# Sending one more batch of strided attention output through DRAM and a DMA transpose, with an earlier deadline

## The chip, the cores and the metric

The kernel runs on one core of a Trainium2 chip. The metric is device time in microseconds. Profiles are single executions. Their times count from the start of the span, which is a little shorter than the timed run. With one core there is no second die to compare with: the label only says that a run took over 1.5% more than the fastest run of the same kernel.

## The reference

Sparse attention with 8 batches, 8 heads, 576 positions and head size 64. Heads 0 to 3 use a local mask, heads 4 to 7 a strided one. Its output x is 4608 x 512 and goes through two matrix products:

```python
rel = pos[:, None] - pos[None, :]
mask_local = (rel >= 0) & (rel < 32)
mask_strided = (rel >= 0) & (pos[None, :] % 32 == pos[:, None] % 32)
attn = softmax(where(mask, q @ k.T / 8, -1e9));  x = attn @ v   # heads side by side
h = x @ w_in            # 512 -> 2048
out = (relu(h) ** 2) @ w_out   # 2048 -> 512
```

## The kernel before

The two-layer part works on chunks of 512 tokens. Each chunk has 16 groups of four matmuls for the first layer (`mm1`) and 16 for the second (`mm2`). From chunk 3 on, the first layer of chunk c alternates with the second layer of chunk c - 1, so a chunk takes 32 groups. Chunk b is the first to need batch b. Attention steps are strewn between the groups so that each batch is done by a deadline. The hooks (`at(n, ...)`) start the loads of later batches at given groups.

A strided unit (two heads) leaves its x with tokens on partitions, and the first layer needs it transposed, in `xt`. The kernel has two ways to do that:

```python
    def step_E(u):                       # on TensorE: 8 transposes, then a copy out of PSUM
        ...
        for t in range(n):
            nc.tensor.transpose(px[:, w * t:w * (t + 1)], x[:, 2 * t:2 * t + 2, :]..., ident[0:w, 0:w])
        dst = xt[p][:, b * S:(b + 1) * S]
        copy = nc.scalar.copy if u < 12 else nc.vector.tensor_copy
        ...
    XD = 6
    def by_dram(u):                      # strided units of batches XD and later
        return not is_local(u) and units[u][0] >= XD

    def step_X(u):                       # by DRAM: write x, six groups later transpose it with a DMA
        b, p = units[u]
        t = dram.tile([S, 2 * D], BF16, name="x_d")
        nc.sync.dma_start(out=t.rearrange("(p j) c -> p (j c)", j=NJ), in_=st.pop(u)["x"]...)
        later(6, lambda: nc.sync.dma_start_transpose(out=xt[p][:, b * S:(b + 1) * S], in_=t))
```

The deadline and the loads hang on the same constant:

```python
    def plan(b, n0, g0, g1):             # loads of batch b; for b >= 4:
        ...
        g = g0 + (g1 - g0) * 45 // 100
        at(g, lambda: loads_qk(b))                                   # q, k and the casts to DRAM
        at(max(g + 8, g0 + (g1 - g0) * 8 // 10), lambda: transpose_str(b))   # L161
        at(n0, lambda: loads_v(b))
        for i in range(2):
            at(g + 14 + 4 * i, lambda u=4 * b + i: transpose_local(u))       # L173
    ...
        g_end, s_end = ready.get(b, starts[b] - (14 if b >= XD else 2)), ends[4 * b + 3]
        ...
        if b + 2 < B:
            plan(b + 2, g_end + 2, g_prev, g_end)
```

So the deadline of batch b also decides when batch b + 2 is loaded. From batch 2 on, the plain q, k and v loads, the x writes, all DMA transposes and all output stores but one last half are issued by SyncE, in program order. The casts of q and k to DRAM and the casts in SBUF are GpSimd's.

The softmax here doesn't subtract the row's maximum and nothing guards it: scores larger than these inputs give would overflow.

Of the kernel before, what the change touches and what calls it, by code (L numbers as in the profile page):

```python
# [14 lines left out]
def kernel(  # L15
# [79 lines left out]
    def is_local(u):  # L95
        return units[u][1] < H // 4
# [356 lines left out]
                                  px.rearrange("c (j p) -> c p j", j=NJ))  # L453
        st.pop(u)

    XD = 6

    def by_dram(u):
        return not is_local(u) and units[u][0] >= XD

# [294 lines left out]
    for b in range(1, B):  # L755
        g_end, s_end = ready.get(b, starts[b] - (14 if b >= XD else 2)), ends[4 * b + 3]
        if b == 1:
# [48 lines left out]
```

## Time and profile before

| | before |
|---|---|
| time, median of 6 runs | 315.38 us (314.51 to 317.44) |
| span of the profiled run | 311.4 us |
| TensorE busy | 96% |
| chain of waits that ended last | TensorE 82%, DMA 7% |

TensorE is the bound, and the DMA engines are nearly full until about 187 us. The lines that carry this are in the prediction. There, ph and py groups are `mm1` and `mm2` (L480 and L498), L444 the x transposes on TensorE, L464 and L466 the x write and its DMA transpose. In SyncE's queue, L107 are the loads of q and k, L185 and L201 the loads of v, L161 the transposes of strided q and k, L173 those of local q and k, L437 those of local x, and L510 the output stores.

### The profile page before, as it was taken

What the parts mean: (1) busy time and instruction counts of PE and PEld (TensorE: products, weight loads), DVE (VectorE), ACT (ScalarE), POOL (GpSimd) and SP (SyncE); (2) the same over time, 40 slices, a digit from 0 to 9 for tenths busy, and PEclk for the clock granted to TensorE, in tenths of its full rate; (3) what the DMA queues carried; (4) which work ended last, traced back from release to release, by engine and by line L of the source; (5) the groups of instructions that cost most, each with busy time, mean ns of one, the idle gap of its engine ahead of it and who ended that gap; (6) DMA issues with size and microseconds to landing.
All of it is one profiled execution on the core that took longest, in us unless ns stands there. A gap on an engine that the chain in (4) does not pass through costs nothing.

```text
span 311.4 us, 6122 instructions
## 1 busy us (share of the span) xinstructions
PE 297.9 (96%) x2309; PEld 147.9 (47%) x2352; DVE 164.5 (53%) x411; ACT 162.8 (52%) x337; POOL 91.5 (29%) x117
## 2 busy tenths in 40 slices
PE   8889989999999999999999999999999999999994
PEld 3444545544555545454454545444444444444441
DVE  6775456468866876577468656654432222222200
ACT  3947746577545765554555565555434444444311
POOL 8527863726830813291048025000000000000000
PEclk9979999999999999999999999999999999999999
DMA  8999999999999999999899886224131000000111
GB/s 148 153 207 204 212 188 257 190 273 232 192 197 222 229 186 170 173 251 226 146 206 196 187 183 132 72 72 55 53 104 56 34 37 34 34 34 36 67 67 67
DMA packets 92172, 44.99 MB, mean 144 GB/s; under 512 B 76592, under 2 KB 85456, under 8 KB 91952
## 3 DMA queue, kind: packets, MB, share of 16 engines
q1 hardware_dynamic: 77120, 34.09, 52.0%
q0 software_dynamic: 14880, 10.39, 23.1%
q8 instruction: 18, 0.29, 0.4%
q10 hardware_dynamic: 144, 0.13, 0.1%
q14 instruction: 10, 0.08, 0.1%
HBM read 36.70 MB, written 13.57 MB: 161 GB/s over the span
## 4 chain that ended last, share of the span: by engine, by line
PE 82%; DMA 7%; POOL 4%; DVE 3%; issue 2%; ACT 1%; DVEq 0%; POOLq 0%
PE ph L480 35%; PE py L498 27%; PE ph L498 11%; DMA w_in_b<-in_moe_w_in_dram 4%; PE pt L412 4%; PE pt L314 3%; DMA qT_s<-in_q_dram 3%; DVE x_s L427 1%; PE pt L270 1%; PE pt L444 1%; POOL w_in_b L233 0%; POOL kT_s L133 0%; DVE kTl L285 0%; POOL w_out_b L237 0%; DVE rinv L426 0%
## 5 line engine op out<-in xcount | busy, mean ns | idle before, releaser
L480 PE MATMUL ph<-xt,w_in_b 128*128 128x512 bf16 x558 | 142.5, 380 | 1.2 <-issue 0.3
L486 ACT ACTIVATE r<-ph 128x512 bf16<-128x512 f32 x143 | 85.3, 597 | 94.4 <-PE ph L480 90.6
L487 DVE TENSOR_TENSOR g_sb<-r 128x512 bf16<-128x512 bf16 x144 | 68.5, 478 | 105.2 <-ACT r L486 104.6
L498 PE MATMUL py<-w_out_b,g_sb 128*128 128x512 bf16 x379 | 99.8, 379 | 1.1 <-issue 0.3
L480 PEld LDWEIGHTS <-w_in_b 128*128 128x128 bf16 x576 | 52.3, 98 | 56.4 <-issue 0.5
L498 PEld LDWEIGHTS <-g_sb 128*128 128x128 bf16 x576 | 52.4, 98 | 55.2
L319 ACT ACTIVATE e<-pt 128x288 bf16<-128x288 f32 (+1 forms) x128 | 47.4, 407 | 13.5 <-PE pt L314 13.4
L498 PE MATMUL ph<-w_out_b,g_sb 128*128 128x512 bf16 x170 | 41.8, 379 | 0.6 <-issue 0.3
L412 PEld LDWEIGHTS <-e 128*128 128x128 bf16 (+1 forms) x392 | 20.9, 97 | 16.2 <-DVE e L325 0.8
L192 POOL CAST vl<-vl_st 128x768 bf16<-128x768 f32 x12 | 11.1, 925 | 50.3 <-DMA vl_st<-in_v_dram 50.1
L427 DVE TENSOR_TENSOR x_s<-pt,rinv 72x384 bf16<-72x384 f32 (+1 forms) x42 | 21.4, 509 | 1.4
L123 POOL CAST q_l<-q_st 96x768 bf16<-96x768 f32 x14 | 13.1, 937 | 24.9 <-DMA q_st<-in_q_dram 24.5
L325 DVE TENSOR_TENSOR e<-e,mask_loc 128x576 bf16<-128x576 bf16 x32 | 18.7, 586 | 2.4 <-ACT e L319 2.4
L509 ACT COPY y<-py 128x512 f32<-128x512 f32 x25 | 14.6, 585 | 5.7 <-PE py L498 5.4
L123 POOL CAST k_l<-k_st 96x768 bf16<-96x768 f32 x14 | 14.3, 1024 | 10.6 <-DMA k_st<-in_k_dram 9.8
L325 DVE TENSOR_TENSOR e<-e,mask_str 72x576 bf16<-72x576 bf16 x32 | 15.5, 490 | 3.1 <-ACT e L319 3.1
L426 DVE RECIPROCAL rinv<-pt 96x6 f32<-96x6 f32 (+2 forms) x70 | 12.8, 183 | 7.9 <-PE pt L412 7.9
L427 DVE TENSOR_TENSOR x_l<-pt,rinv 96x384 bf16<-96x384 f32 x28 | 15.5, 553 | 1.0
L509 ACT COPY y<-ph 128x512 f32<-128x512 f32 x10 | 5.9, 585 | 17.4 <-PE ph L498 17.4
L208 POOL CAST vs<-v_st 72x1024 bf16<-72x1024 f32 x12 | 13.4, 1146 | 0.4
L412 PE MATMUL pt<-vs,e 72*128 72x65 bf16 x224 | 13.1, 193 | 0.1
L523 PE MATMUL py<-y 128*128 128x512 bf16 x22 | 9.6, 523 | 1.3 <-DVE y L652 1.3
(87 smaller groups left out, 159.0 us busy)
## 6 DMA issues: line engine op xcount, KB each, us to landing
out_dram<-y SPq DMA_DIRECT2D x35, 256.0 KB, 3.4
vl_st<-in_v_dram SPq DMA_DIRECT2D x24, 144.0 KB, 3.4
v_st<-in_v_dram SPq DMA_DIRECT2D x12, 288.0 KB
q_st<-in_q_dram SPq DMA_DIRECT2D x16, 144.0 KB, 4.6
k_st<-in_k_dram SPq DMA_DIRECT2D x16, 144.0 KB, 5.8
w_in_b<-in_moe_w_in_dram POOLq DMA_DIRECT2D x4, 512.0 KB, 12.8
w_out_b<-in_moe_w_out_dram POOLq DMA_DIRECT2D x4, 512.0 KB, 10.5
q_st<-in_q_dram SPq DMA_DIRECT2D x7, 288.0 KB, 9.9
```

What stands on the lines that cost most here:

```text
L123: copy(t.rearrange("p j h d -> p h j d"), s[name + "f"].rearrange("p h (j d) -> p h j d", j=6))
L208: (copy or nc.gpsimd.tensor_copy)(t[:, :, 0:D], s["vf"].rearrange("p h (j d) -> p (h j) d", d=D))
L319: nc.scalar.activation(e[0:kn, lo:lo + S // 2], banks[row][half][0:kn, 0:S // 2], AF.Exp, scale=scale)
L325: nc.vector.tensor_tensor(x, x, m.to_broadcast([kn, n, w]), op=ALU.mult)
L412: nc.tensor.matmul(po[:, n - n0, :], e[0:kn, pos(n):pos(n) + 128], rhs[0:kn, src(n), 0:D + 1], start=True, stop=True)
L426: nc.vector.reciprocal(rinv[0:w, 0:m], po[0:w, 0:m, D:D + 1])
L427: nc.vector.tensor_tensor(x, po[0:w, 0:m, 0:D], rinv[0:w, 0:m].to_broadcast([w, m, D]), op=ALU.mult)
L480: nc.tensor.matmul(ph, w_in_b[:, kk, 128 * ff:128 * (ff + 1)], xt[kk][:, 512 * c:512 * (c + 1)], start=(kk == order[0]), stop=(kk == order ...
L486: nc.scalar.activation(r, ph, AF.Relu)
L487: later(1, lambda: nc.vector.tensor_tensor(g[:, ff, :], r, r, op=ALU.mult))
L498: nc.tensor.matmul(py, g[:, ff, 128 * j:128 * (j + 1)], w_out_b[:, ff, :], start=(ff == 0), stop=(ff == 15))
L509: nc.scalar.copy(y, py)
```

## The change

The intent is to take 16 transposes and two copies of batch 5 from TensorE and VectorE. As x then has a longer way, batch 5's attention gets the deadline that batches 6 and 7 have: 14 groups before its chunk instead of 2.

```diff
-    XD = 6
+    XD = 5
```

## The prediction

> **What bounds the kernel now.** I read the page first, then the chain of waits, then TensorE's timeline through the stage of batches 5 and 6, and then the timeline of SyncE's DMA queue over the same stretch. From the page of the kernel before:
>
> ```profile
> span 311.4 us, 6122 instructions
> PE 297.9 (96%) x2309; PEld 147.9 (47%) x2352; DVE 164.5 (53%) x411; ACT 162.8 (52%) x337; POOL 91.5 (29%) x117
> DMA  8999999999999999999899886224131000000111
> L444 PE MATMUL pt<-ident,x_s 72*128 72x72 bf16 x80 | 4.8, 197 | 1.0 <-DVE x_s L427 0.8
> ```
>
> The first two lines say that TensorE is busy 96% of the span. The chain of waits that ended last is 82% TensorE. So an instruction taken from TensorE in the middle of the run is worth its own slot, and no more. The third line has slices of 311.4 / 40 = 7.8 us: the DMA engines are 80 to 90% busy until slice 24, about 187 us. The change works just before that point. The fourth line holds the transposes the change removes (16 of 80, those of batch 5). TensorE's timeline shows what they cost on the path:
>
> ```profile
> 165.56 1.03 PE L498 MATMUL py<-w_out_b,g_sb 128*128 128x512 bf16 x4
> 166.43 0.42 PE L444 MATMUL pt<-ident,x_s 72*128 72x72 bf16 x8
> 166.69 1.03 PE L480 MATMUL ph<-xt,w_in_b 128*128 128x512 bf16 x4
> ...
> 176.55 0.34 PE L412 MATMUL pt<-vl,e 128*128 128x65 bf16 x6
> 176.73 1.03 PE L480 MATMUL ph<-xt,w_in_b 128*128 128x512 bf16 x4
> ```
>
> Columns are start, extent, engine, line, operands, count. Groups of four matmuls start 0.865 us apart (166.43 - 165.56 = 0.87), and a block of eight transposes moves the next group by 166.69 - 166.43 = 0.26 us. There are no holes here. Counted in the built order, the L480 group at 176.73, just after batch 6's first L412 block, is group 144. It is the first of chunk 5, which is the first to read batch 5's x. In the kernel before, the second x copy of batch 5 runs on VectorE from 175.02 to 175.78, just in time for that group's fourth matmul near 177.4, with no DMA. The change puts that x behind SyncE's queue, so that queue decides:
>
> ```profile
> 164.60 1.28 SPq L437 DMA_TRANSPOSE xt<-x_l  x1
> 165.97 0.52 SPq L510 DMA_DIRECT2D out_dram<-y  x1
> 171.12 1.46 SPq L161 DMA_TRANSPOSE qT_s<-q_d  x1
> 172.67 1.58 SPq L161 DMA_TRANSPOSE kT_s<-k_d  x1
> 174.34 0.53 SPq L510 DMA_DIRECT2D out_dram<-y  x1
> 174.97 1.23 SPq L173 DMA_TRANSPOSE qT<-q_l  x1
> ...
> 180.83 2.99 SPq L185 DMA_DIRECT2D vl_st<-in_v_dram  x4
> 183.87 0.90 SPq L201 DMA_DIRECT2D v_st<-in_v_dram  x2
> ```
>
> See the hole from 166.49 to 171.12, then 13 us with hardly a gap. This is batch 7's loading. The queue's own waits over 166 to 172 us name the hole:
>
> ```profile
> SPq L161 <- DMA q_d<-in_q_dram: 4.6, 1, 4.6
> ```
>
> The queue stands still until batch 7's cast of q to DRAM has landed. GpSimd issues that cast at 165.16, only after casting batch 6's v.
>
> **What the Trainium skill says.** "Perfetto Trace Analysis", section "DMA Instruction — HWDGE (DVE, Sync)", puts the semaphore wait in the sequencer before the reported start, and frees it for the next instruction only at the reported end. The trace agrees: nothing was issued in the 4.6 us. "DMA: Bandwidth & Descriptors", section "Two DMAs through the same engine are not ordered", says a DMA that reads what an earlier one wrote must wait for the completion semaphore. The built program has that wait between x's write (L464) and its transpose (L466). The issue times fit but do not show it. "TensorE: Matmul & The Clock Gate", section "What's actually happening", says about 3.4 us of idleness halves the array clock, and about 3.4 us of activity restores it. The trace agrees on the size of a half-clock stretch: TensorE was sparsely used just before 16 us, and granted clock over 16-18, 18-20 and 20-22 us was 0.85, 0.50 and 0.79, which adds up to 3.4 us at half clock:
>
> ```profile
> 18.00:20.00 2.00, 2.00 (x25) 1.27 (x23) 1.59 (x5) 0.70 (x2) 0.34 (x1) 0.50 1.24 206
> ```
>
> (The last three columns are granted clock, DMA share and GB/s.)
>
> **The change part by part.** It removes, for two units of batch 5, 16 transposes and two 128x576 copies. On TensorE that is 2 x 0.26 = 0.52 us on the path. The copies (about 0.75 us each on VectorE, 53% busy) lie beside other work and give nothing.
>
> It adds two writes x_d<-x_s and two transposes xt<-x_d. Batch 6's show SyncE issue times of 0.33 and 1.18 us, and the transpose lands 2.6 us after issue when DMA is quiet. Batch 6's x_l transposes had a median of 5.1 in the busy stretch.
>
> It moves batch 5's attention from groups 110-142 to 110-130, batch 6's from 142-162 to 130-162, and batch 7's loads earlier: q and k from group 124 to 119, their strided transposes from 135 to 127, v from 144 to 132. The squeeze itself costs nothing that I can see: batch 6 has run in 20 groups without a hole. Of batch 6's work, three more product blocks and one more unit's scores now precede group 144: 3 x 0.18 us and one of about 0.5, so 1.0 us. These only move from after it to before it. Group 144 starts near 176.7 - 0.5 + 1.0 = 177.2 us, and its fourth matmul, which needs the second x, 3 x 0.22 later, near 177.9.
>
> Now the built issue order on SyncE, with the waits of the kernel before. The order is unchanged until batch 6's v loads at 155 us. Batch 7's q and k, an output and two x_l transposes follow as before, and the first x write is issued near 165.6. Then the two L161 transposes stand in line **before the second x write**. Their wait is q_d, and GpSimd's order, which sets q_d, has not changed. So the hole still ends near 171.1. From there the queue issues, in this order: two L161, output, second x write, first x transpose, six v loads, two L173, output, and only then the second x transpose. Durations with gaps, from the rows above: 1.55 + 1.67 + 0.61 + 0.40 + 1.25 + 3.04 + 1.00 + 1.32 + 1.32 + 0.60 = 12.76 us. The second x transpose is issued at 171.1 + 12.8 = 183.9. I choose 4.5 us for landing, between 2.6 and 5.1 and near the latter, because the v loads just before it are in flight. So x lands near 188.4.
>
> The stall at group 144 is 188.4 - 177.9 = 10.5 us, on the path, because TensorE takes its matmuls in order. It is longer than 3.4 us, so the array comes back at half clock for about 3.4 us: 1.7 us lost, an estimate from the half-clock stretch above. Sum: 315.67 - 0.5 + 10.5 + 1.7 = 327.4 us.
>
> **The rivals.** *The transfer is hidden, as intended.* Fourteen groups are 14 x about 1 us, and for batch 6 it worked: second write at 196.13, transpose at 202.38, next chunk at 209.08. Against it: batch 6's queue has no later batch to load, while batch 5's stands in batch 7's. This would give 315.67 - 0.5 = 315.2.
>
> *A short stall of 2 to 5 us,* if q_d lands earlier, or the L161 wait falls in a quieter queue. The order is fixed and 12.8 us of issue remain, so the hole would have to end near 165 us, before GpSimd has even issued the cast at 165.16. With 1.7 for the clock, if it is hit at all, this would give 317 to 322.
>
> *A longer stall,* if the DMA engines bind and not the issue. Between 155 and 190 us the hardware queue's packets alone take
>
> ```profile
> q1 hardware_dynamic: 16480, 6.08, 95.2%
> ```
>
> of the 16 engines' time, and the change adds four transfers there. Landing could be 7 or 8 us: 330 to 331.
>
> *VectorE or ScalarE becomes the bound in the squeezed stretch:* about half busy in the page; batch 6 speaks against it. At most 1 us.
>
> **Range and chances.** The predicted time is 327.4 us. The low end, 322.4, is the queue 5 us faster than I add up; the high end, 331.4, is a landing 4 us later. Faster by over 2% (below 309.4) has nothing behind it, as only 0.5 us is removed: 0.01. Within 2% (up to 322.0) needs the stall to be under about 5 us (322.0 - 315.2 - 1.7): 0.11. Slower by over 2%: 0.88.
>
> **What would show it.** Right: TensorE has one hole of 8 to 14 us near 178 us, ahead of an L480 group waiting for DMA xt<-x_d. SyncE shows the L161 wait for q_d of 4 to 5 us ahead of the second L464, and the second batch-5 L466 starts near 184. The clock is 0.5 for about 3.4 us after the hole. L444 falls from 80 to 64, and the page's row of slices has a hole in PE near slice 23. Wrong: if the second L464 is issued before 168 us, or the hole ahead of L161 is gone, the stall shrinks to the first rival's. If TensorE stalls earlier than group 144, an input of batch 5 or 6 was late, and I have missed a wait.

## The result, and the profile after

| | before | after |
|---|---|---|
| time, median of 6 runs | 315.38 us | 326.14 us (324.43 to 328.15) |
| span of the profiled run | 311.4 us | 324.9 us |
| chain of waits: TensorE, DMA | 82%, 7% | 62%, 20% |
| x transposes on TensorE (L444, x_s) | 80 | 64 |

The ratio is 1.0339, with a 95% interval of 1.0285 to 1.0393. Ratios are the mean time of one kernel's fast runs over that of the other's of the same rounds, so not quite the ratio of the medians. From the page of the kernel after:

```profile
PE   8889898999899999999999169999999999999994
PEclk9999999999999999999999859999999999999999
...
L480 PE MATMUL ph<-xt,w_in_b 128*128 128x512 bf16 x572 | 144.9, 381 | 9.9 <-DMA xt<-x_d 9.6
```

Each digit is a slice of 324.9 / 40 = 8.1 us. The 23rd and 24th digits (179 to 195 us) are 1 and 6 in TensorE's row, a hole where 9 is usual, and 8 and 5 in the granted clock. Before the change the L480 row had 1.2 us of idleness and none of it from a DMA; now 9.6 us wait for x's DMA transposes. TensorE's timeline of the kernel after shows where:

```profile
179.08 0.59 PE L480 MATMUL ph<-xt,w_in_b 128*128 128x512 bf16 x2
181.21 0.38 PE L480 MATMUL ph<-xt,w_in_b 128*128 128x512 bf16 x1 [1.53 <-DMA xt<-x_d]
189.67 0.58 PE L480 MATMUL ph<-xt,w_in_b 128*128 128x512 bf16 x1 [8.09 <-DMA xt<-x_d]
190.19 0.70 PE L314 MATMUL pt<-qT_s,kT_s 64*72 64x72 bf16 x16
190.82 1.89 PE L498 MATMUL py<-w_out_b,g_sb 128*128 128x512 bf16 x4
```

One group of four is torn into 2 + 1 + 1. It is group 144, the first of chunk 5. Its third matmul waits for the first strided x of batch 5 and its fourth for the second. Between them TensorE ran nothing: no later matmul overtook the waiting one in those 8.1 us. Afterwards a group takes 1.7 us instead of 0.87 (190.82 to 192.50). SyncE's queue in the same stretch:

```profile
168.19 0.52 SPq L464 DMA_DIRECT2D x_d<-x_s  x1
171.38 2.73 SPq L161 DMA_TRANSPOSE qT_s<-q_d  x1
174.65 1.28 SPq L161 DMA_TRANSPOSE kT_s<-k_d  x1
176.02 0.54 SPq L510 DMA_DIRECT2D out_dram<-y  x1
176.65 0.34 SPq L464 DMA_DIRECT2D x_d<-x_s  x1
177.09 1.20 SPq L466 DMA_TRANSPOSE xt<-x_d  x1
178.38 2.29 SPq L185 DMA_DIRECT2D vl_st<-in_v_dram  x4
180.76 0.85 SPq L201 DMA_DIRECT2D v_st<-in_v_dram  x2
181.73 1.21 SPq L173 DMA_TRANSPOSE qT<-q_l  x1
183.05 1.21 SPq L173 DMA_TRANSPOSE kTl<-k_l  x1
184.68 0.37 SPq L510 DMA_DIRECT2D out_dram<-y  x1
185.11 1.21 SPq L466 DMA_TRANSPOSE xt<-x_d  x1
```

The second x write stands behind batch 7's L161, and its transpose behind six v loads and two L173. The second transpose is issued at 185.11, and TensorE's fourth matmul starts 4.56 us later. The hole, the clock and the removed transposes add up to 9.6 + 1.8 - 0.5 = 10.9 us, where 1.8 is the clock's share, taken from the filled-hole experiment below. The medians differ by 326.14 - 315.38 = 10.8. That this is so close is in part chance: 9.6 is the hole of one profile, and two more profiles of the change (below) have 6.8 and 7.4. The two profiles here differ by more, 13.5 us. Group 144 started at 179.08, and 1.9 us of that is beyond the 177.2 worked out from the profile of before, whose run (313.14 us) was itself 2.2 us faster than its median. The last 0.7 us is not accounted for.

### The profile page after: what moved, and what is told of

The parts are those of the page before. It is cut to its first block, busy times and chain, and to the rows that moved or that the text cites.

```text
span 324.9 us, 6145 instructions
## 1 busy us (share of the span) xinstructions
PE 301.7 (93%) x2336; PEld 147.1 (45%) x2336; DVE 165.3 (51%) x409; ACT 163.0 (50%) x337; POOL 91.4 (28%) x117
## 2 busy tenths in 40 slices
DMA packets 93556, 45.58 MB, mean 140 GB/s; under 512 B 77832, under 2 KB 86696, under 8 KB 93336
## 4 chain that ended last, share of the span: by engine, by line
PE 62%; DMA 20%; POOL 5%; DVE 5%; SPq 3%; issue 2%; ACT 1%; POOLq 0%; DVEq 0%; ACTq 0%
PE ph L480 27%; PE py L498 23%; PE ph L498 8%; DMA vs<-in_v_dram 4%; DMA w_in_b<-in_moe_w_in_dram 4%; DMA qT_s<-in_q_dram 3%; PE pt L314 2%; PE pt L412 2%; DMA k_d<-in_k_dram 2%; DMA vl_st<-in_v_dram 2%; DVE x_s L427 2%; DMA k_st<-in_k_dram 2%; SPq L173 1%; DMA xt<-x_d 1%; DMA kTl<-k_l 1%
## 5 line engine op out<-in xcount | busy, mean ns | idle before, releaser
L480 PE MATMUL ph<-xt,w_in_b 128*128 128x512 bf16 x572 | 144.9, 381 | 9.9 <-DMA xt<-x_d 9.6
L498 PE MATMUL py<-w_out_b,g_sb 128*128 128x512 bf16 x400 | 103.6, 381 | 0.0
L480 PEld LDWEIGHTS <-w_in_b 128*128 128x128 bf16 x576 | 52.7, 98 | 59.2 <-issue 3.4
L498 PE MATMUL ph<-w_out_b,g_sb 128*128 128x512 bf16 x176 | 42.8, 379 | 0.0
L192 POOL CAST vl<-vl_st 128x768 bf16<-128x768 f32 x12 | 11.5, 956 | 53.8 <-DMA vl_st<-in_v_dram 40.1
L325 DVE TENSOR_TENSOR e<-e,mask_loc 128x576 bf16<-128x576 bf16 x32 | 19.6, 613 | 2.4 <-ACT e L319 2.4
L325 DVE TENSOR_TENSOR e<-e,mask_str 72x576 bf16<-72x576 bf16 x32 | 17.1, 540 | 3.1 <-ACT e L319 3.1
L426 DVE RECIPROCAL rinv<-pt 96x6 f32<-96x6 f32 (+2 forms) x70 | 12.8, 182 | 8.9 <-PE pt L412 8.9
L123 POOL CAST k_l<-k_st 96x768 bf16<-96x768 f32 x14 | 13.1, 938 | 8.2 <-DMA k_st<-in_k_dram 8.1
L208 POOL CAST vs<-v_st 72x1024 bf16<-72x1024 f32 x12 | 13.5, 1148 | 0.4
L314 PEld LDWEIGHTS <-kT_s 64*72 64x72 bf16 x192 | 4.6, 118 | 13.7 <-issue 13.1
## 6 DMA issues: line engine op xcount, KB each, us to landing
w_out_b<-in_moe_w_out_dram POOLq DMA_DIRECT2D x4, 512.0 KB, 10.9
```

The costliest lines, as they stand in the source:

```text
L123: copy(t.rearrange("p j h d -> p h j d"), s[name + "f"].rearrange("p h (j d) -> p h j d", j=6))
L208: (copy or nc.gpsimd.tensor_copy)(t[:, :, 0:D], s["vf"].rearrange("p h (j d) -> p (h j) d", d=D))
L325: nc.vector.tensor_tensor(x, x, m.to_broadcast([kn, n, w]), op=ALU.mult)
L426: nc.vector.reciprocal(rinv[0:w, 0:m], po[0:w, 0:m, D:D + 1])
L480: nc.tensor.matmul(ph, w_in_b[:, kk, 128 * ff:128 * (ff + 1)], xt[kk][:, 512 * c:512 * (c + 1)], start=(kk == order[0]), stop=(kk == order ...
L498: nc.tensor.matmul(py, g[:, ff, 128 * j:128 * (j + 1)], w_out_b[:, ff, :], start=(ff == 0), stop=(ff == 15))
```

## The experiments

Two theories stood at first. **Order:** x comes late because of what stands ahead of it in SyncE's queue. **Full engines:** x comes late because the DMA engines have more to move in that stretch, whatever the order. A third suspect was the squeeze of batch 5 into 20 groups.

**The early deadline alone.** The deadline and batch 7's early loads stay, and batch 5's x is transposed on TensorE as before.

```diff
-        return not is_local(u) and units[u][0] >= XD
+        return not is_local(u) and units[u][0] >= 6
```

> The early deadline alone (batch 5's attention in 20 groups, batch 7's loads early), with batch 5's x still transposed on TensorE. Queue theory: no x of batch 5 waits in SyncE's queue, so no hole at group 144; 315 to 316.5 us, within 0.4% of before. Rival (the squeeze or the early loads are what costs): near 326 us, with the hole still there.

Measured: 315.64 us median, ratio 1.0022 (0.9998 to 1.0045). No first-layer matmul waits for x. The squeeze and the early loads cost nothing that can be told from noise.

**Batch 7's loads back at their old groups**, x still by DRAM.

```diff
-            plan(b + 2, g_end + 2, g_prev, g_end)
+            plan(b + 2, *((144, 110, 142) if b == 5 else (g_end + 2, g_prev, g_end)))
```

> The change, but with batch 7's loads put back to the groups at which the kernel before issues them (q and k 124, strided transposes 135, local transposes 138 and 142, v 144). Now both x writes and the first x transpose stand before the two L161 transposes in SyncE's queue; only the second x transpose stands behind them. Queue theory: second x transpose issued about 7 us earlier than in the change (near 177 to 178 instead of 185.1), hole at group 144 of 2 to 4 us in all, 317 to 320 us. Rival (the DMA engines are full, the same bytes move in the same stretch): hole of 7 us or more, 323 us or more.

Measured: 317.74 us median of 12 runs (313.16 to 321.17), ratio of the fast runs 1.0034. The profile fell in a run labelled slow (320.07 us), with one wait of 3.7 us for x. Most of the loss is gone. The second x transpose was issued at 179.87 there, some 2 us later than expected. The runs scatter widely: six of the 12 are slow, and the ratio leaves them out. Whether all six had such a wait is not known, since only one was profiled. So the ratio of the fast runs may flatter this kernel; the median holds all 12.

**The strided transposes behind x as well.** As the last one, and L161 at group 138.

```diff
-        at(max(g + 8, g0 + (g1 - g0) * 8 // 10), lambda: transpose_str(b))
+        at(138 if b == 7 else max(g + 8, g0 + (g1 - g0) * 8 // 10), lambda: transpose_str(b))
```

> As the run with the loads put back, but batch 7's strided transposes L161 at group 138, so that they too stand behind the second x transpose. The bytes are the same. Queue theory: second x transpose issued near 174, landed near 178, hole of 0 to 1 us, 315 to 316.5 us (0.5 us of removed transposes against a rest of the hole). Rival (DMA engines full): still 5 us or more of hole, over 320 us.

Measured: 315.5 us median of 20 runs, ratio 0.9998 (0.9974 to 1.0022). SyncE's queue in this kernel:

```profile
169.23 0.66 SPq L464 DMA_DIRECT2D x_d<-x_s  x1
174.38 1.17 SPq L466 DMA_TRANSPOSE xt<-x_d  x1
...
176.27 1.18 SPq L466 DMA_TRANSPOSE xt<-x_d  x1
177.56 1.32 SPq L161 DMA_TRANSPOSE qT_s<-q_d  x1
```

The second x transpose is issued at 176.27 instead of 185.11 (some 2 us later than expected), group 144 starts at 180.01, and TensorE waits for no x:

```profile
180.01 1.03 PE L480 MATMUL ph<-xt,w_in_b 128*128 128x512 bf16 x4
```

The change and this kernel move the same 45.58 MB in the same 93556 packets. What differs is the order of issue, and with it when each transfer runs, and the loss is gone. That shows the place in the queue as the cause, against the theory that the order does not matter. It does not part SyncE's issue time from the load on the DMA engines: with the v loads, their bytes too went behind x (DMA share over 170 to 180 us 0.71, against 0.99 in the change). The 0.5 us that the removed transposes should bring lies within the interval, so it is neither shown nor excluded. This is the best version with batch 5 by DRAM, and it is level with the kernel before. None of the versions run here beats both.

**The cast earlier.** The wait ahead of L161 is for batch 7's cast to DRAM, so I moved that to the front of GpSimd's order.

```diff
+        if b < 7:                 # in loads_qk
             cast_str_dram(b)
 ...
+        if b == 7:                # in plan
+            at(108, lambda: cast_str_dram(b))
```

> The change with its issue order on SyncE as it is, but batch 7's casts of q and k to DRAM moved to the front of GpSimd's order (group 108, ahead of batch 6's v), so that L161 finds its data landed. Queue theory: the wait of 2.6 us before L161, most of its 2.7 us of issue and the 0.5 us before the second one fall away, 3.5 to 5 us in all, so the hole shrinks from 9.6 to about 5 us: 320 to 322.5 us. Rival (full DMA engines set the landing whatever the issue order): unchanged near 326 us.

Measured: 328.89 us median of 4 runs (327.31 to 329.55), ratio 1.0433. This expectation failed: the kernel is slower than the change. SyncE's queue:

```profile
174.45 0.50 SPq L464 DMA_DIRECT2D x_d<-x_s  x1
175.06 1.30 SPq L161 DMA_TRANSPOSE qT_s<-q_d  x1
...
187.15 1.72 SPq L466 DMA_TRANSPOSE xt<-x_d  x1
```

The wait is gone, exactly as meant: 0.1 us between the first x write and L161. But that write is issued at 174.45 instead of 168.19, 6.3 us later, which is more than the wait was. Batch 6's local transposes began 2.6 us later than in the change (150.91 against 148.32), before the cast can have mattered much: it was issued at 147.71. The queue already lagged at one transpose of a local x (L437), which held it for 5.72 us from 139.65, against 2.70 from 140.14 in the change; why, no run shows. TensorE waited 1.4 us for a local x there, before the cast was issued, so that part of this kernel's time isn't the cast's. The rest came while the cast's transfer ran: those four transposes took up to 2.91 us of issue each, against at most 1.38, and the v loads behind them began at 160.51 instead of 154.34. Here, moving one transfer forward went with everything behind it moving back.

**The cast left out.** To take away both wait and transfer, batch 7's L161 read batch 6's cast. Its output is wrong, which doesn't matter for the time. The comparison with the reference still passed, so its tolerance doesn't see this error.

```diff
+            if b == 7:
+                big[b, name] = kept[name]
+                continue
```

> Wrong result on purpose: the change without batch 7's casts of q and k to DRAM; its strided transposes L161 read batch 6's casts, which landed long before. Wait and transfer are both gone, the order on SyncE is as in the change. If the wait for the cast (2.6 to 5 us in the profiles of the change) was on the path to x: second x transpose near 179 to 181 instead of 183 to 185, hole of 3 to 6 us, 319 to 322.5 us. If the queue was only standing still while the DMA engines worked off their backlog, and the v loads ahead of x are what counts: 323 us or more, as in the change.

Measured: 323.75 us median of 4 runs, ratio 1.0254 (1.0188 to 1.0319). The change, run beside it for the third time (below), had 326.52. From SyncE's queue (line numbers are 4 higher in this kernel):

```profile
168.03 1.45 SPq L468 DMA_DIRECT2D x_d<-x_s  x1
169.57 1.31 SPq L165 DMA_TRANSPOSE qT_s<-q_d  x1
...
181.75 1.16 SPq L470 DMA_TRANSPOSE xt<-x_d  x1
```

No wait, and the second x transpose comes 1.9 us earlier than in the change beside it (183.64), with a hole of 5.1 instead of 7.4 us. By the two medians, the wait and the cast's transfer together are worth 2.8 us. That size is uncertain: the intervals of the two ratios overlap (the change's is 1.0257 to 1.0386), and the change's second repetition, in another round, had 323.81. The result falls between the two theories: the hole (3 to 6 us) is as the first foretold, the time (323 us or more) as the second, and the transpose's issue lies between them. What is clear is that the greater part of the loss remains without them.

**Only the v loads and local transposes behind x.** L161 stays ahead.

```diff
-        at(n0, lambda: loads_v(b))
+        at(138 if b == 7 else n0, lambda: loads_v(b))
 ...
-            at(g + 14 + 4 * i, lambda u=4 * b + i: transpose_local(u))
+            at((140 if b == 7 else g + 14) + 4 * i, lambda u=4 * b + i: transpose_local(u))
```

> The change with batch 7's v loads at group 138 and its local transposes at 140 and 144, so that they stand behind the second x transpose; the L161 transposes and their wait stay ahead of the second x write. Issue-order theory: the second x transpose no longer waits for six v loads and two L173 but only for its own write to land, so it is issued near 181 to 182 instead of 185 and lands near 185 to 186: hole of 5 to 7 us, 321 to 324 us. Rival (only the total of the DMA engines' work up to then counts, not the order): 326 us.

Measured: 316.86 us median of 20 runs (313.77 to 324.04), ratio of the fast runs 1.0035 (1.0009 to 1.0061). Better than I expected (321 to 324 us). Seven of the 20 runs are slow. The profile fell in a run labelled slow, with a wait for x of 4.1 us in two parts, so how the typical run does without is not seen.

**Only L161 behind x.** The line of the strided-transposes experiment alone.

> The change with only batch 7's strided transposes L161 moved behind the second x transpose (group 138); v loads and two L173 stay ahead of it. Issue-order theory: the wait for the cast is no longer ahead of x, but the first x transpose now waits for its write to land, then v loads and L173: second x transpose near 181 to 183, hole of 5 to 8 us, 321 to 325 us. Neither this run nor the one with the v loads moved should reach the 315.5 us of the run with both moved.

Measured: 323.59 us median of 4 runs, ratio 1.0281, hole 7.35 us, second x transpose at 182.05:

```profile
175.10 2.18 SPq L185 DMA_DIRECT2D vl_st<-in_v_dram  x4
...
182.05 1.68 SPq L466 DMA_TRANSPOSE xt<-x_d  x1
```

As expected. Of the two things that stand ahead of x, the v loads and local transposes are the dear ones, and L161 with its wait the cheap one.

**The hole filled with matmuls.** To see the clock's share, 40 matmuls that nobody reads before group 144.

```diff
+    def fill():
+        pw = ps_t.tile([128, 512], FP32, name="pt")
+        for _ in range(40):
+            nc.tensor.matmul(pw, w_in_b[:, 0, 0:128], w_in_b[:, 0, 0:512], start=True, stop=True)
+    at(144, fill)
```

> The change, with 40 matmuls of 128x512 that nobody reads (40 x 0.216 = 8.6 us) on TensorE just before group 144, where it otherwise waits some 9.6 us for x. Clock theory: the wait stays, hidden under them, but TensorE is idle for only about 1 us, so the clock stays at full speed and the 2.1 us lost at half clock after the wait come back: about 2 us less than the change run beside it, granted clock 0.99. Rival (the half clock costs nothing on the path): the same time as the change, or more.

Measured: 325.14 us median of 6 runs, ratio 1.0339. The change beside it:

> The change as it is, beside these runs on the same chip: 324.5 to 328 us, hole of 8 to 11 us at group 144, as measured before.

Measured for the change again (no edit): 323.81 us median of 4 runs (323.66 to 326.44), hole 6.8 us, both a little below what was expected. So the fill saved no time, and the expectation failed as put. In the profiled run of the filled kernel x came later than in the change beside it: its transpose was issued at 185.73 instead of 183.24, and the fourth matmul of group 144 started 1.9 us later (189.04 instead of 187.11), which used up what the clock gave back. Whether the fill or chance made it later is not known; the change's own three profiles spread from 183.2 to 185.1. The timelines still part the two effects. First the filled kernel, then the change again (its lines are numbered one higher):

```profile
179.59 8.80 PE L757 MATMUL pt<-w_in_b 128*128 128x512 bf16 x40
188.22 1.20 PE L480 MATMUL ph<-xt,w_in_b 128*128 128x512 bf16 x4
...
198.03 1.03 PE L480 MATMUL ph<-xt,w_in_b 128*128 128x512 bf16 x4
```

```profile
187.11 0.59 PE L481 MATMUL ph<-xt,w_in_b 128*128 128x512 bf16 x1 [6.84 <-DMA xt<-x_d]
...
197.94 1.03 PE L481 MATMUL ph<-xt,w_in_b 128*128 128x512 bf16 x4
```

Between the fourth matmul of group 144 and the same later group lie 197.94 - 187.11 = 10.83 us in the change, and 198.03 - 189.04 = 8.99 us in the filled kernel (189.04 is the group's end, 188.22 + 1.20, less the 0.38 us of its last matmul; the group lasts 1.20 us instead of 1.03 because that matmul still waited 0.17 us for x). The difference, 1.8 us, is the half clock. Granted clock over the span was 0.997 and 0.977.

**A shorter fill**, 30 matmuls, with the change beside it again.

> The change with 30 unread matmuls (30 x 0.216 = 6.5 us) before group 144, less than the hole this time. Clock theory: x lands when it did, TensorE is idle for only 0 to 3 us, the clock stays up, 1.5 to 2 us less than the change beside it. Rival (half clock costs nothing): equal to the change.

> The change as it is, for the run with the shorter fill: 323.5 to 328 us, hole of 7 to 10 us, granted clock about 0.98.

Measured: 326.61 us median of 6 (ratio 1.0367), and 326.52 for the change (322.62 to 332.06, ratio 1.0321). This failed too: group 144 came early in the profiled run, the fill left 4.3 us of idleness, and the clock was halved all the same. Nothing follows from it, except that even the rest of the hole is enough.

**The profiles of state fast together.** Take the start of the fourth matmul of group 144 from each profile with x by DRAM, and subtract it from the span:

| kernel | second x transpose issued | fourth matmul of group 144 | rest of the span |
|---|---|---|---|
| strided transposes behind x (no wait) | 176.27 | 180.66 | 133.3 |
| hole filled, 40 matmuls | 185.73 | 189.04 | 133.3 |
| hole filled, 30 matmuls | 184.31 | 188.86 | 135.5 |
| cast left out | 181.75 | 186.88 | 135.3 |
| only L161 behind x | 182.05 | 186.23 | 135.8 |
| change, second time | 183.24 | 187.11 | 135.1 |
| change, third time | 183.64 | 188.45 | 135.9 |
| change | 185.11 | 189.67 | 135.2 |
| cast earlier | 187.15 | 192.03 | 135.8 |

The rest of the span is the same within 0.8 us wherever the clock dropped, and 1.8 to 2.6 us less in the two where it did not. So wherever there is a hole, the time is set by when the second x of batch 5 arrives, and nothing later gives any of it back.

## Why the prediction was right

The predicted 327.4 us stand against 326.14. Step by step:

- *What it removes.* L444's x_s transposes fell from 80 to 64, as foretold. Their 0.5 us could not be seen in any time.
- *The squeeze costs nothing.* Right, by the run with the deadline alone.
- *The hole is at group 144, for x.* Right: 9.6 us in the change's profile, 6.8 and 7.4 in its two repetitions, against 10.5 and a band of 8 to 14. The repetitions lie below the band, mainly because group 144 started later than foretold, and less because x came earlier: the group started at 179.1, 179.5 and 180.3 instead of 177.2, and its fourth matmul, set by x, at 189.7, 187.1 and 188.4 against 188.4.
- *The sum.* It added a stall worked out from a fast run's profile (313.14 us) to a median (315.67, of the three runs then at hand). On the profile's own base it gives 313.14 - 0.5 + 10.5 + 1.7 = 324.8 us; the three medians of the change are 326.14, 323.81 and 326.52. The mechanism was right, and so was the size within about 2 us, but that 327.4 lies only 1.3 from 326.14 is in part luck.
- *Second x transpose at 183.9, landing 4.5 us later.* Measured 185.1, 183.2 and 183.6, and the matmul 4.6, 3.9 and 4.8 us after it. The sum of issue times was sound because it came from the same instructions in the same kind of stretch.
- *The clock, 1.7 us.* Measured 1.8 us in the filled-hole pair, and 1.8 to 2.6 us by the table of all fast profiles: slightly too low.
- *The wait of 4 to 5 us for q_d ahead of L161.* The profile after has 2.6 us for q_d and 0.5 us for k_d, and the hole between the entries, 168.71 to 171.38, was 2.7 us. It was smaller because the queue came to it 2.2 us later (first x write at 168.19 instead of 165.6) and left it at nearly the foretold time. In the repetitions the wait for q_d was 4.5 and 3.3 us. Its end, which is what the sum rests on, came at 171.4, 170.4 and 171.4, against 171.1.

One argument of the prediction doesn't hold as put. Among its signs of being wrong it says that if the hole ahead of L161 is gone, the stall shrinks to the first rival's, which is none. In two runs that hole was gone, and a stall of 5.1 us (cast left out) and of 11.5 us in two parts (cast earlier) was still there. The prediction's own sum says as much: 12.8 us of issue remain behind the hole. Taking the cast away brought about 2.8 us (uncertain, see above), and moving it forward cost 2.8 (328.89 against 326.14, from different rounds). While the queue stood still, the DMA engines did not: from 168.7 to 171.4 us of the change's profile they moved 183 GB/s. In these runs what makes x late is the sum of what was issued ahead of it, and the wait is the smaller part.

The third rival, a longer stall because full engines make the landing take 7 or 8 us, did not come true: x's reader started 3.9 to 4.8 us after issue. How much of the cost of standing behind the v loads is SyncE's issue time, and how much the load on the engines, stays open: every edit here moved both, and no run gave x's transposes a queue of their own. Full engines aren't enough as a cause by themselves: with the same bytes over the run and x ahead of the v loads, the hole is gone. (A small misreading: the prediction calls the DMA engines 80 to 90% busy up to slice 24, but a digit 9 stands for 90% or more.)

## What to carry to other kernels

When work moves from a busy engine to a DMA queue, read that queue's timeline at the place where the new transfers will stand, and add up what is ahead of them. A deadline given in groups of matmuls does not help if the queue is further behind than the matmuls are, as here with 14 groups. If the transfer comes late, move it ahead of loads that are not needed yet, before trying to shorten single waits: here the order was worth 10.6 us (326.14 against 315.5), and the one wait that caught the eye, with the transfer behind it, about 2.8, which is uncertain.

## What the Trainium skill lacked or had wrong

- "DMA: Bandwidth & Descriptors", section "Issuing engines are not separate DMA queues", says the sequencer's time to initiate a DMA "is usually small relative to the DMA itself". Here a DMA transpose held SyncE for 1.2 to 2.7 us in the stretch shown of the profile after, while x's transposes landed 4.1 to 4.3 us after issue. Such times added up: 8.5 us went by from the second x write to the issue of its transpose (176.65 to 185.11).
- No page that I read gives a landing time of a DMA transpose under load. The same 576 x 128 transpose from DRAM landed a median of 2.6 us after issue where the engines were quiet (batches 6 and 7 before the change), and in the three profiles of the change its reader started 3.9 to 4.8 us after issue where they were full.
- "TensorE: Matmul & The Clock Gate", section "What's actually happening", puts both the fall and the return of the clock after about 3.4 us. The length of the half clock agrees: 10.2 us in the profile after (183.6 to 193.9), three times 3.4. The section does not say how much work inside such a window counts as busy. In the profile with only the v loads and local transposes behind x, no idle stretch was longer than 2.43 us (a second one of 1.64 us came after a single matmul), and the clock was still at half for 3.4 us (granted clock 0.96 over 182 to 186 us, 0.62 over 186 to 190).
